# Output projection of a token pair: seven products of quadrant sums in place of eight, weight operands streamed from DRAM

## The chip, the cores and the metric

The kernel runs on one core of a Trainium2 chip. The metric is the device time of one execution in microseconds (us); the median of a few executions is compared. The core's engines run in parallel, each through its own instruction queue in order: TensorE (PE, with PEld for its weight loads), VectorE (DVE), ScalarE (ACT), GpSimd (POOL) and SyncE (SP), which here only issues DMAs.

## The reference

Two linear-attention blocks over the same 2048 tokens (D = 576, 32 heads of 18), mixed by a gate:

```python
def _A_ref(x, wqkv, wo):            # phi(t) = where(t > 0, t + 1, exp(t)) + 1e-6
    kv = einsum("bhsd,bhse->bhde", phi(k), v);  z = phi(k).sum(s)
    o = einsum("bhqd,bhde->bhqe", phi(q), kv) / (phi(q) . z + 1e-6)
    return o.reshape(B, S, D) @ wo
def _B_ref(x, wqkv, w_phi, wo):     # phi(t) = [softmax(t @ w_phi), softmax(-t @ w_phi)] per head
    return (same linear attention).reshape(B, S, D) @ wo
g = sigmoid((x * gate_w).sum(-1))
return g * A + (1 - g) * B
```

## The kernel before, in words

The 2048 tokens are 16 tiles of 128, worked on in pairs. Three stages follow each other: keys and values of block A, keys and values of block B, then the queries of both with the output projection. All matrix products are exact to float32 by splitting each operand into a high and a low part (`split`: ACT copies the high part, DVE or POOL subtracts it for the low one) and multiplying high by high, high by low and low by high. The projections of x already run in seven products of quadrant sums (`strassen`), with x and its sums kept in DRAM and fetched for each pair (`x_fetch`).

The last stage is the loop over `i` at the end of the kernel. In block `i` it merges three sequences by weight: `q_units(i + 1)` (query projection of the next pair: seven units), `tr_units` (transposes of the normalised queries of pair `i` by TensorE) and `out_units` (output projection of pair `i - 1`). `norm` runs at the head of the block, and `num` multiplies the transposed features of block B by its folded key-value matrix. `out_units` of before takes one tile and one half of the 576 output columns at a time: nine row chunks (`ath`/`atl`, `oh`/`ol` are the high and low left operands) times three matmuls of 128x128 by 128x288. Its weights are resident: `WO(s, i)` reads five tiles (`WOt`) that `load_out` fetched once from the DRAM tensors `wod` and `mad`, which `prep_wo`, `prep_out` and `join_out` filled during the stage before.

No order is written out by hand: the code lists the operations, and `Plan` gives each a due time and an order per engine from costs and from when buffers come free (`order`, `run`). So an edit moves instructions on all engines. Tiles named `op` have eleven buffers (`op_tile`); seven hold the query weights (`WQ`) through the last stage. In a row of the profile all operations carry line 354, the line of `emit` that issues them, so they are told apart by tile names.

Of the kernel before, what the change touches and what calls it, by code (L numbers as in the profile page):

```python
# [18 lines left out]
P = 128  # L19
# [339 lines left out]
def tile_gated_mix(ctx, tc, xT, wAk, wAv, wBv, wAq, wkT, wqT, phi, woA, woB, out):  # L359
# [524 lines left out]
    def prep_wo():  # L884
        for i in range(6):
            src = row_tile()[:, :D]
            SP.dma_start(src, woB[:, i, :])
            if i % 2 == 0:
                t = op_tile()
            k = 2 * (i % 2)  # L890
            split(src, t[:, k], t[:, k + 1], G)
            if k:
                SP.dma_start(WO_d[:, i - 1:i + 1], r(t).rearrange("p (i s) n -> p i s n", i=2))
            yield

# [14 lines left out]
    WO_d = dr.tile([P, 6, 2, D], F32, name="wod")  # L910
# [23 lines left out]
    MA_d = dr.tile([D, 2, D], F32, name="mad")  # L934

    def prep_out():
# [27 lines left out]
        for c in range(6):  # L964
            wo, nxt = nxt, load(c + 1) if c < 5 else None
            here = [(a, 2 * c + a) for a in range(2 if c < 5 else 1)]
            k, rows = 2 * (c % 2), 64 * len(here)
            if c == 4:
                two = rr(wk.tile([P, 2, D], F32, name="st", bufs=1))
                hi_lo = two[:, 0], two[:, 1]  # L970
            elif c == 5:
                hi_lo = rr(area[0][:, 1152:1152 + D]), rr(area[1][:, :D])
            else:
                if c % 2 == 0:
                    t = op_tile()
                hi_lo = t[:, k], t[:, k + 1]
# [7 lines left out]
            hv, lv = [v[:rows].rearrange("p (a c) -> p a c", a=2) for v in hi_lo]  # L984
            A.activation(hv, pm[:rows, :, :HB], AF.Copy)
            V.tensor_tensor(lv, pm[:rows, :, :HB], r(hv), op=ALU.subtract)
            if c < 4:
                if c % 2:
                    dst = MA_d[108 * (c - 1):108 * (c + 1)].rearrange("(c a q) s n -> a q c s n", c=2, a=2)
                    for a in range(2):  # L990
                        SP.dma_start(dst[a], r(t[64 * a:64 * a + 54]).rearrange("p (c s) n -> p c s n", c=2))
            elif c == 4:
                for a, gr in here:
                    SP.dma_start(MA_d[54 * gr:54 * gr + 54], r(two[64 * a:64 * a + 54]))
            else:
                for s, v in enumerate(hi_lo):
                    SP.dma_start(MA_d[540:, s], r(v[:36]))
            yield

    def join_out():  # L1000
        for a in range(2):
            plan.after(1)
            SP.dma_start(WO_d[64 * a + 54:64 * a + 64, 0:5], MA_d[378:478].rearrange("(k a q) s n -> a q k s n", a=2, q=10)[a])
        plan.after(1)
        SP.dma_start(WO_d[36:, 5], MA_d[478:570])
# [28 lines left out]
    def both():  # L1034
        yield from prep_wo()
        yield from prep_q1()
        yield from prep_out()
        yield from prep_q2()

    prep = both()  # L1040
    a_done, pend = pend, []
    for n in range(NT // 2):
# [6 lines left out]
        for i, _ in enumerate(strassen(x, WB, TB, HB, two_banks, lambda: uws[0][:, 0], *b_sinks(n, uws, pend))):  # L1049
# [11 lines left out]
            if n + i > 3:  # L1061
                steps(prep)
            if n == NT // 2 - 1 and i == 2:
                join_out()
# [5 lines left out]
    def load_out(k, at):  # L1070
        t = op_tile() if k < 4 else tail_tile()
        WOt[k] = t
        plan.first = at
        if k < 3:
            SP.dma_start(r(t).rearrange("p (i s) n -> p i s n", i=2), WO_d[:, 2 * k:2 * k + 2])
        elif k == 3:
            to = r(t).rearrange("p (i s) n -> p i s n", i=2)
            SP.dma_start(to[:126], MA_d[:252].rearrange("(g p) s n -> p g s n", g=2))
            SP.dma_start(to[126:], MA_d[570:574].rearrange("(g p) s n -> p g s n", g=2))
        else:  # L1080
            SP.dma_start(r(t[:126]), MA_d[252:378])
            SP.dma_start(r(t[126:]), MA_d[574:])

    WOt = {}

    def WO(s, i):
        return WOt[i // 2][:, 2 * (i % 2) + s]
# [75 lines left out]
    def q_units(n, x, uws, c1_tile, then={}):  # L1163
# [29 lines left out]
    def tr_units(t, at, uT):  # L1193
        f, ub = qs.pop(t)
        ath, atl = at
# [17 lines left out]

    def num(uT, at, last):
        ath, atl = at
        oh, ol = ot = [wk.tile([P, KT, 256], F32R, name="vo") for _ in range(2)]
# [10 lines left out]
        for m, p1 in enumerate(pms):  # L1227
            j = 2 * m
            n = 2 if j < 4 else 1
            src = p1[:, :256 * n].rearrange("p (j n) -> p j n", n=256)  # L1230
            A.activation(oh[:, j:j + n], src, AF.Copy)
            V.tensor_tensor(ol[:, j:j + n], src, r(oh[:, j:j + n]), op=ALU.subtract)
            if n == 1:
                A.activation(ath[:64, 3], p1[:64, 256:], AF.Copy)
                V.tensor_tensor(atl[:64, 3], p1[:64, 256:], r(ath[:64, 3]), op=ALU.subtract)
        return ot

    def out_units(t, blk):
        ath, atl = blk["at"]
        oh, ol = blk["ot"]  # L1240
        c = slice(P * (t % 2), P * (t % 2) + P)
        osb = row_tile()[:, :D]
        dst = out[P * at_row(t):P * at_row(t) + P]
        for hf in range(2):
            po = bank_tile()
            cc = slice(HB * hf, HB * hf + HB)
            srcs = [(ath, atl, m, 6 + m) for m in range(3)] + [(oh, ol, j, j) for j in range(KT)] + [(ath, atl, 3, 5)]
            st = []
            for hi, lo, j, i in srcs:
                st += [(hi[:, j, c], WO(0, i)), (hi[:, j, c], WO(1, i)), (lo[:, j, c], WO(0, i))]  # L1250
            for i, (l, w) in enumerate(st):
                PE.matmul(po[:, :HB], l, w[:, cc], start=(i == 0), stop=(i == len(st) - 1))
            A.activation(osb[:, cc], po[:, :HB], AF.Copy)
            if t >= NT - 2:
                SP.dma_start(dst[:, cc], osb[:, cc])
            if hf == 0:
                yield
        if t < NT - 2:
            SP.dma_start(dst, osb)
        yield  # L1260
# [24 lines left out]
    for i in range(NT // 2 + 1):  # L1285
# [4 lines left out]
        if i and i <= NT // 2:  # L1290
            prev["ot"] = num(uT, prev["at"], i >= NT // 2 - 1)
        if i + 1 < NT // 2:
            x = x_fetch(pairs[i + 1])
            if i == 0:
                load_out(3, x["dma"])
                load_out(4, x["dma"])
            if i == 1:
                for k, m in enumerate((1, 4, 6)):
                    load_out(k, x["dma"][m:m + 1])
            uws = [extra_uw if i == 0 else uw_tile(), uw_tile()]  # L1300
            seqs.append((7, .7, q_units(i + 1, x, uws, row_tile)))
# [5 lines left out]
        if i:  # L1307
            seqs.append((4, 1, chain(*[out_units(t, prev) for t in (2 * i - 1, 2 * i - 2)])))
# [83 lines left out]
```

## Time and profile before

| what | value |
|---|---|
| median of 3 runs | 561.49 us (561.21 to 562.13) |
| profiled execution | 562.4 us, span of its instructions 560.7 us |
| PE busy | 551.6 us (98%), 4584 matmuls |
| DVE, ACT, POOL busy | 421.8 (75%), 288.3 (51%), 245.8 us (44%) |
| TensorE clock granted | 1.00 throughout |
| DMA | 96.22 MB, mean 172 GB/s |
| last stage | from about 285 us to the end |

A row of a group reads: line, engine, operation, output tile <- input tiles, shapes, count | busy us, mean ns of one | idle time of the engine ahead of it and what ended it. Matmuls overlap each other, so the mean of one (297 ns) is its latency; the step from one to the next is read from the timeline.

### The profile page before, as it was taken

To read this page: it belongs to the slowest core of one execution; us is meant where nothing else is said; L and a number is where in the kernel's file an instruction comes from. 1 tells how busy PE (TensorE), PEld (TensorE's weight loads), DVE (VectorE), ACT (ScalarE), POOL (GpSimd) and SP (SyncE) were. 2 spreads that over 40 slices of the span, in tenths; PEclk is the share of its full clock that TensorE was granted. 3 is DMA by queue.
4 is the path that set the end of the run, shared out by engine and by line. 5 is a ranking of instruction groups with operands and counts; after the bars stand their busy time and mean duration, and the time that the engine had idled before them with its cause. 6 is when DMAs were issued, how large, how long until landed. Compare 5 with 4: busy or idle time off the path is not lost.

```text
span 560.7 us, 11695 instructions
## 1 busy us (share of the span) xinstructions
PE 551.6 (98%) x4584; PEld 527.7 (94%) x4584; DVE 421.8 (75%) x673; ACT 288.3 (51%) x602; POOL 245.8 (44%) x218
## 2 busy tenths in 40 slices
PE   8999999999999999999999989999999999999997
PEld 8999999999999978999998989898999989899897
DVE  5872678843897997899889998769597795978810
ACT  6666687655645544543355645435443544535421
POOL 6575487632793523363228764214152332424200
PEclk9999999999999999999999999999999999999999
DMA  8739767976759566757759622132322314100001
GB/s 282 272 116 312 252 236 253 338 245 269 273 208 384 184 214 210 250 184 261 284 182 311 247 80 77 48 105 70 106 78 85 97 44 122 51 1 23 31 34 43
DMA packets 38625, 96.22 MB, mean 172 GB/s; under 512 B 4198, under 2 KB 7782, under 8 KB 37034
## 3 DMA queue, kind: packets, MB, share of 16 engines
q1 hardware_dynamic: 38570, 95.47, 50.2%
q8 instruction: 36, 0.59, 0.4%
q14 instruction: 19, 0.16, 0.1%
HBM read 59.64 MB, written 36.70 MB: 172 GB/s over the span
## 4 chain that ended last, share of the span: by engine, by line
PE 83%; DVE 10%; POOL 2%; ACT 2%; issue 1%; DMA 1%; SPq 0%; POOLq 0%; DVEq 0%; ACTq 0%
PE pq L354 35%; PE tr L354 25%; PE bk L354 23%; DVE row L354 3%; DVE dd L354 2%; DVE den L354 1%; DVE mm L354 1%; DVE ss L354 1%; POOL late L354 1%; POOL row L354 1%; DVE at L354 1%; DMA at<-xT 1%; DVE rs L354 1%; ACT row L354 1%; ACT uw L354 0%
## 5 line engine op out<-in xcount | busy, mean ns | idle before, releaser
L354 PE MATMUL pq<-op,x 128*128 128x288 f32 (+1 forms) x636 | 102.6, 297 | 0.0
L354 PEld LDWEIGHTS pq<-op,x 128*128 128x128 f32 x636 | 90.4, 189 | 0.9 <-issue 0.4
L354 PE MATMUL bk<-op,vo 128*128 128x288 f32 x480 | 71.0, 297 | 0.0
L354 PE MATMUL pq<-tail,x 128*128 128x288 f32 (+1 forms) x308 | 66.9, 300 | 0.0
L354 PEld LDWEIGHTS bk<-op,vo 128*128 128x128 f32 x480 | 65.8, 188 | 0.2 <-DVE vo L354 0.2
L354 PE MATMUL pq<-op,xp 128*128 128x288 f32 (+1 forms) x336 | 54.0, 297 | 0.0
L354 PE MATMUL bk<-op,at 128*128 128x288 f32 x288 | 51.3, 301 | 0.0
L354 POOL TENSOR_TENSOR row<-row,z_a 128x576 f32<-128x576 f32 x16 | 22.9, 1429 | 63.3 <-issue 35.7
L354 PEld LDWEIGHTS pq<-tail,x 128*128 128x128 f32 x308 | 49.1, 188 | 1.3 <-issue 0.6
L354 ACT ACTIVATE row<-bk 128x288 f32<-128x288 f32 x38 | 15.6, 411 | 64.4 <-PE bk L354 64.4
L354 PEld LDWEIGHTS pq<-op,xp 128*128 128x128 f32 x336 | 47.5, 188 | 0.2
L354 ACT ACTIVATE row<-row,epsc 128x576 f32<-128x576 f32 x54 | 41.9, 777 | 10.5 <-DVE row L354 9.4
L354 POOL TENSOR_TENSOR row<-row,den 128x378 f32<-128x378 f32 (+1 forms) x32 | 24.6, 789 | 47.8 <-DVE den L354 39.4
L354 DVE TENSOR_REDUCE ss<-uw 128x64 f32<-128x1152 f32 x23 | 31.0, 1350 | 18.5 <-ACT uw L354 17.9
L354 ACT ACTIVATE row<-tr 128x288 f32<-128x288 f32 (+1 forms) x74 | 30.2, 409 | 28.1 <-PE tr L354 27.2
L354 PEld LDWEIGHTS bk<-op,at 128*128 128x128 f32 x288 | 41.7, 189 | 0.4 <-issue 0.4
L354 ACT ACTIVATE uw<-uw 128x1152 f32<-128x1152 f32 x23 | 26.8, 1166 | 23.8 <-DVE uw L354 13.6
L354 POOL TENSOR_TENSOR x<-at,x 128x384 fp32r<-128x384 f32 (+2 forms) x35 | 31.3, 898 | 16.5 <-ACT x L354 14.4
L354 DVE TENSOR_TENSOR row<-row,pq 128x576 f32<-128x576 f32 (+1 forms) x30 | 22.5, 750 | 18.7 <-ACT row L354 14.3
L354 PE MATMUL tr<-op,xv 128*128 128x288 f32 (+1 forms) x204 | 33.7, 302 | 0.0
L354 ACT ACTIVATE uT<-tr 118x512 f32<-118x512 f32 (+1 forms) x48 | 25.9, 559 | 14.6 <-PE tr L354 14.5
L354 DVE TENSOR_TENSOR vo<-row,pq 128x540 f32<-128x540 f32 (+1 forms) x56 | 22.8, 449 | 11.4 <-ACT row L354 10.4
(206 smaller groups left out, 1264.3 us busy)
## 6 DMA issues: line engine op xcount, KB each, us to landing
xp<-s0x SPq DMA_DIRECT2D x12, 512.0 KB
at<-xT SPq DMA_DIRECT2D x18, 320.0 KB
x<-x1x SPq DMA_DIRECT2D x12, 384.0 KB
x<-s2x SPq DMA_DIRECT2D x12, 384.0 KB
s0x<-xp SPq DMA_DIRECT2D x8, 512.0 KB
out<-row SPq DMA_DIRECT2D x14, 288.0 KB
op<-wb SPq DMA_DIRECT2D x3, 1152.0 KB
wod<-op SPq DMA_DIRECT2D x3, 1152.0 KB
```

Source lines behind the costliest of these rows:

```text
L354: fn(*[a.real() if isinstance(a, View) else a for a in args], **{k: v.real() if isinstance(v, View) else v for k, v in kw.items()})
```

## The change

The output projection of a pair is now taken as one product of a 256-token operand by the weights, both cut into quadrants, with seven products of quadrant sums in place of eight (the last 128 of the operand's rows stand apart as a tail). Per pair that is 7 x 12 matmuls and 12 for the tail, 96, where 2 x 2 x 27 = 108 stood. The left operands' sums and splits are made for each pair: four sums and seven splits, on DVE (`fast`, `slow`) for the first pairs and on POOL later. The seven weight operands (high and low, 1152 KB each) are made during the stage before by `prep_o` into DRAM tensors `od0` to `od3` (`O_d`; the tail is `otd`). The first of them stays resident, and the other six are loaded for every pair into `op` tiles. `prep_wo` and `join_out` are gone, `prep_out` runs first and writes plain rows to `mad`. The scaling of block B's features in `norm` (`scale_ub`) is on DVE for all tiles; it was on POOL for the first four.

The core of the diff:

```diff
+    O_OPS = {1: (0, 0), 2: (1, 0), 3: (1, 1), 5: (2, 0), 6: (2, 1), 7: (3, 0), 4: (3, 1)}
+    O_d = [dr.tile([P, 1 if i == 0 else 2, 2, 4, HB], F32, name=f"od{i}") for i in range(4)]
...
+    def prep_o():
...
+        for k in range(4):
+            r1, r2 = nxt
+            ta, tb = wide[k % 2][:, 2], wide[k % 2][:, 3]
+            G.tensor_tensor(ta[:, :HB], r1[:, HB:], r1[:, :HB], op=ALU.subtract)
+            G.tensor_tensor(ta[:, HB:], r2[:, HB:], ta[:, :HB], op=ALU.subtract)
+            put_two(2, k, ta, None)
             yield
...
     def both():
-        yield from prep_wo()
+        yield from prep_out()
         yield from prep_q1()
-        yield from prep_out()
         yield from prep_q2()
+        yield from prep_o()
...
+    def load_o(op):
+        t = op_tile()
+        i, o = O_OPS[op]
+        SP.dma_start(r(t).rearrange("p a b -> p (a b)"), O_d[i][:, o].rearrange("p s k c -> p (s k c)"))
...
-            norm_b(t, *qb[t], ub, (G, V, G if t < 4 else V))
+            norm_b(t, *qb[t], ub, (G, V, V))
...
-        src = chunks(p1)
-        A.activation(ath[:, 0:4, c], src, AF.Copy)
-        V.tensor_tensor(atl[:, 0:4, c], src, r(ath[:, 0:4, c]), op=ALU.subtract)
+        A.activation(ra[:, :, c], chunks(p1), AF.Copy)
...
+    def out_units(i, blk, wo):
+        fast = V if i < 3 or i >= NT // 2 - 1 else G
+        slow = V if i < 2 else G
...
+        L12 = cut(a12, vo(), V)
+        fast.tensor_tensor(s1, a21, a22, op=ALU.add)
+        slow.tensor_tensor(a21, a11, a21, op=ALU.subtract)
+        fast.tensor_tensor(a11, s1, a11, op=ALU.subtract)
+        slow.tensor_tensor(a12, a12, a11, op=ALU.subtract)
+        LS2 = cut(a11, slots[1], fast)
+        LS1 = cut(s1, vo(), slow)
+        split(d, own[:, 0, 2048:2176], own[:, 0, 2176:], V)
...
+        X = bank_tile()
+        mul(X, ops(L11, 1), True)
+        A.activation(ob[0][:, h0], X[:, :HB], AF.Copy)
+        LS3 = cut(a21, slots[0], slow)
+        yield
+        Y = bank_tile()
+        mul(Y, tail(*t1, 0) + ops(L12, 2), True)
+        V.tensor_tensor(ob[0][:, h0], ob[0][:, h0], Y[:, :HB], op=ALU.add)
...
+        mul(X, ops(LS2, 6), False)
...
+        mul(Z, tail(*t2, 1) + ops(LS1, 5), True)
...
+        mul(X, ops(LS3, 7), False)
...
+        mul(X, ops(L22, 4) + tail(*t2, 0), False)
...
+        mul(Z, ops(LS4, 3) + tail(*dd, 1), False)
...
         if i:
-            seqs.append((4, 1, chain(*[out_units(t, prev) for t in (2 * i - 1, 2 * i - 2)])))
+            wo = {op: WO[1] if op == 1 else load_o(op) for op in (1, 2, 6, 5, 7, 4, 3)}
+            seqs.append((7, 1 if i == 6 else 1, out_units(i, prev, wo)))
```

How this stands in the queues is shown at one block in the middle of the last stage, and at the stage's first pair. In the rows, `bk` is an accumulator in PSUM, `at`, `vo` and `row` are operands of the output projection, `x...`, `xp`, `xv` are the fetched operands of the query projection, and the numbers tell buffers apart.

On PE before, at the fourth unit of the query projection in that block (`pq` is its accumulator), one half tile of the output projection begins with resident weights `op_3729`, `tail_3733`, `op_3754`:

```order
L354 MATMUL pq_4831<-op_3371,x3_4675 128x288 x12
L354 MATMUL tr_5071<-ident_138,row_4925 128x128 x4
L354 MATMUL bk_5080<-op_3729,at_4517 128x288 x5
L354 MATMUL pq_4831<-op_3415,xv_4707 128x288 x6
L354 MATMUL pq_4831<-tail_2567,x2_4282 128x288 x2
L354 MATMUL pq_4831<-op_3415,xv_4707 128x288 x6
L354 MATMUL pq_4831<-tail_2567,x2_4282 128x288 x2
L354 MATMUL bk_5080<-op_3729,at_4517 128x288
L354 MATMUL bk_5080<-tail_3733,at_4517 128x288 x3
```

On PE now, at the same units: the end of product 2 (`op_4912`), product 6 (`op_4988`) and product 5 (`op_5147`).

```order
L354 MATMUL bk_5063<-op_4912,vo_5043 128x288 x4
L354 MATMUL pq_5101<-op_2487,xp_4750 128x288
L354 MATMUL bk_5003<-op_4988,op_4084 128x288 x12
L354 MATMUL tr_5164<-ident_138,late_3932 118x128 x3
L354 MATMUL pq_4919<-op_3385,x3_4766 128x288 x12
L354 MATMUL bk_5191<-tail_3896,row_5036 128x288 x3
L354 MATMUL pq_4919<-op_3406,xv_4823 128x288 x4
L354 MATMUL bk_5191<-op_5147,vo_5072 128x288 x12
```

Between two readings of resident tiles nothing had to arrive; now each product reads a tile loaded for it. After product 5 stand 12 matmuls of the query projection, four transposes and seven matmuls more, and then on PE now products 7 (`op_5171`), 4 (`op_5235`) and 3 (`op_5293`):

```order
L354 MATMUL bk_5003<-op_5171,op_4084 128x288 x12
L354 MATMUL pq_5101<-tail_2496,x4_4881 128x288
L354 MATMUL pq_5101<-op_3431,x4_4881 128x288 x6
L354 MATMUL pq_5101<-tail_2496,x4_4881 128x288 x2
L354 MATMUL tr_5303<-ident_138,late_3932 118x128 x4
L354 MATMUL tr_5311<-ident_138,late_3932 118x128 x4
L354 MATMUL bk_5003<-op_5235,vo_5145 128x288 x12
L354 MATMUL bk_5003<-tail_3896,row_5036 128x288 x3
L354 MATMUL tr_5343<-ident_138,late_3932 118x128 x3
L354 MATMUL pq_5351<-op_2434,xu_4949 128x288 x12
L354 MATMUL pq_5373<-op_2446,x1_5070 128x288 x2
L354 MATMUL bk_5191<-op_5293,op_4084 128x288 x12
```

On SP before, the same stretch of the block holds fetches of x and a store of `out` only:

```order
L354 DMA x1_4969<-x1x3_662 128x768
L354 DMA xp_5023<-s0x3_713 128x1024
L354 DMA out<-row_4940 128x576
L354 DMA x3_5078<-s1x3_751 128x512
L354 DMA xv_5110<-x2x3_800 128x512
L354 DMA x2_5116<-x3x4_875 128x256
L354 DMA x4_5175<-s2x3_826 128x768
```

On SP now:

```order
L354 DMA x1_5070<-x1x3_662 128x768
L354 DMA op_5147<-od2_3039 128x2304
L354 DMA xp_5153<-s0x3_713 128x1024
L354 DMA op_5171<-od3_3090 128x2304
L354 DMA x3_5197<-s1x3_751 128x512
L354 DMA op_5235<-od3_3090 128x2304
L354 DMA xv_5250<-x2x3_800 128x512
L354 DMA x2_5257<-x3x4_875 128x256
L354 DMA op_5293<-od1_3180 128x2304
L354 DMA x4_5309<-s2x3_826 128x768
```

Four weight loads have come between the fetches of x. Of the eleven `op` buffers seven hold query weights, one the first weight operand and one (`op_4084`) left operands, so two are left for the loads: `op_5147` takes the buffer of `op_4912`, `op_5171` that of `op_4988`, `op_5235` that of `op_5147`, `op_5293` that of `op_5171`.

On DVE before, behind the first product of block B's features (`num`), stand the subtractions that give the low parts (`vo<-tr`, `vo<-bk`, `at<-tr`) among the norms:

```order
L354 TENSOR_TENSOR vo_4162<-tr_4055,vo_4089 128x512
L354 TENSOR_TENSOR vo_4162<-tr_4056,vo_4089 128x512
L354 TENSOR_REDUCE ss_4177<-uw_3976 128x64
L354 RECIPROCAL rs_4193<-ss_4177 128x64
L354 TENSOR_TENSOR vo_4162<-bk_4057,vo_4089 128x256
```

On DVE now, in the same place, for the first pair: sums (`st`, `at`) and splits (`vo`, `op_4084`) of the left operands, and the scaling of features (`late`), which POOL did before.

```order
L354 TENSOR_TENSOR op_4084<-at_3944,op_4084 128x512
L354 TENSOR_TENSOR dd_4239<-dd_4239,rs_4179 128x64
L354 SCALAR_TENSOR_TENSOR den_4330<-dd_4239 128x32
L354 TENSOR_TENSOR late_3932<-uw_4015,rs_4155 128x72
L354 RECIPROCAL den_4330<-den_4330 128x32
L354 SCALAR_TENSOR_TENSOR rs_4179<-den_4330,gate_269,rs_4179 128x64
L354 TENSOR_TENSOR late_3932<-vo_3952,rs_4179 128x10x54 x2
L354 TENSOR_TENSOR late_3932<-vo_3952,rs_4179 128x72
L354 TENSOR_TENSOR vo_4275<-st_4216,vo_4275 128x512
L354 TENSOR_TENSOR op_4084<-at_3944,op_4084 128x512
L354 TENSOR_TENSOR row_4325<-row_4325,pq_4260 128x576
L354 TENSOR_TENSOR vo_4361<-at_3944,vo_4361 128x512
```

The low parts of one tile's chunks have given way to sums and splits of 512 columns each for the pair.

More of the change, by code (lines that the diff above doesn't have):

```diff
@@ L998, in prep_out @@
-            yield
[L1000 to L1005, printed above, removed]
+            ma = row_tile()[:, :D]
+            A.activation(ma[:rows].rearrange("p (a c) -> p a c", a=2), pm[:rows, :, :HB], AF.Copy)
+            for a, gr in here:
+                n = 54 if gr < 10 else 36
+                SP.dma_start(MA_d[54 * gr:54 * gr + n], ma[64 * a:64 * a + n])
@@ L1236, in num @@
[L1236 to L1259, printed above, removed]
+        A.activation(ra[:64, 3], pms[2][:64, 256:], AF.Copy)
```

217 lines of the change are left out of this document (139 added, 78 removed).

## The prediction

> **What bounds the kernel now.** I read the page first: how busy each engine is, and which engines make up the chain that ended last.
>
> ```profile
> PE 551.6 (98%) x4584; PEld 527.7 (94%) x4584; DVE 421.8 (75%) x673; ACT 288.3 (51%) x602; POOL 245.8 (44%) x218
> PE 83%; DVE 10%; POOL 2%; ACT 2%; issue 1%; DMA 1%; SPq 0%; POOLq 0%; DVEq 0%; ACTq 0%
> ```
>
> A busy TensorE need not be the bound, so I next asked whom it waited for, and looked at the last stage, which the change rewrites, in stretches from one `num` to the next.
>
> ```profile
> PE tr L354 <- DVE vo L354: 1.8, 2, 1.1
> ...
> core 0: us, PE busy (x) PEld busy (x) DVE busy (x) ACT busy (x) POOL busy (x), PEclk, DMA share, GB/s
> 383.28:417.32 34.04, 34.01 (x261) 32.52 (x261) 26.51 (x48) 15.55 (x31) 11.56 (x11) 1.00 0.27 84
> 451.35:485.38 34.03, 34.02 (x262) 32.53 (x261) 26.47 (x48) 15.66 (x31) 11.52 (x11) 1.00 0.27 80
> ```
>
> The longest wait of TensorE in total is 1.8 us, and block after block of the last stage takes the same 34.04 us with TensorE full. DVE has 7.5 us of slack in a block, POOL 22, and the DMA engines are at 27%. So TensorE bounds each block, at a fixed clock, and whatever matmul goes shortens it, as long as nothing else takes its place. Only at the start of the stage is that otherwise:
>
> ```profile
> 285.00:340.00 55.00, 52.33 (x385) 48.34 (x382) 53.31 (x92) 30.52 (x67) 35.28 (x33) 1.00 0.59 195
> ```
>
> There DVE works 53.3 of 55 us and TensorE loses 2.7.
>
> **What is removed.** The output projection is these three groups:
>
> ```profile
> L354 PE MATMUL bk<-op,vo 128*128 128x288 f32 x480 | 71.0, 297 | 0.0
> L354 PE MATMUL bk<-op,at 128*128 128x288 f32 x288 | 51.3, 301 | 0.0
> L354 PE MATMUL bk<-tail,at 128*128 128x288 f32 x96 | 18.4, 297 | 0.0
> ```
>
> 864 matmuls, 108 for each of eight pairs. Now there are 96 a pair, 768; 96 go. The step of one I take from the end of the run, where nothing but these stands on TensorE, and that of a transpose from a run of eight a little before:
>
> ```profile
> 535.25 1.03 PE L354 MATMUL tr<-ident,late 128*118 128x128 f32 x8
> 536.03 1.04 PE L354 MATMUL bk<-op,at 128*128 128x288 f32 x6
> ...
> 549.73 1.36 PE L354 MATMUL bk<-op,at 128*128 128x288 f32 x9
> ...
> 556.90 0.56 PE L354 MATMUL bk<-op,at 128*128 128x288 f32 x3
> ```
>
> From 549.73 to 556.90 start 54 matmuls: 7.17 / 54 = 0.1328 us each. Eight transposes take 536.03 - 535.25 = 0.78, so 0.098 each. The change removes 96 x 0.1328 = **12.75 us** of TensorE's path, 1.59 a block: a block comes to 34.04 - 1.59 = 32.45 us if nothing is late.
>
> **What is added: the stream of weights.** This is the dispute. Six operands of 1152 KB come from DRAM for each pair, into two rotating buffers. What such a load costs is read from these rows: sizes, then three stretches in which the queue was full, then one load alone.
>
> ```profile
> op<-wq SPq DMA_DIRECT2D x3, 1152.0 KB
> xp<-s0x SPq DMA_DIRECT2D x12, 512.0 KB
> xv<-x2x SPq DMA_DIRECT2D x12, 256.0 KB
> x<-s1x SPq DMA_DIRECT2D x12, 256.0 KB
> x<-x3x SPq DMA_DIRECT2D x12, 128.0 KB
> ...
> DMA packets 1321, 4.04 MB, mean 404 GB/s; under 512 B 145, under 2 KB 145, under 8 KB 1192
> ...
> DMA packets 666, 3.69 MB, mean 369 GB/s; under 512 B 57, under 2 KB 57, under 8 KB 351
> q1 hardware_dynamic: 664, 3.67, 101.1%
> ...
> DMA packets 204, 1.73 MB, mean 346 GB/s; under 512 B 17, under 2 KB 17, under 8 KB 17
> ...
> 119.27 0.33 SPq L354 DMA_DIRECT2D at<-xT  x1
> 122.58 0.43 DVE L354 TENSOR_TENSOR at<-at 128x256 f32<-128x256 f32 x1 [1.37 <-DMA at<-xT]
> ```
>
> The stretches are 168 to 178 us, 263 to 273 (the three loads of query weights, of the same shape as the new ones, with small ones beside them), and 265 to 270 within it. The lone load of 320 KB took 122.58 - 119.27 = 3.31 us from issue to the instruction that waited; 0.33 MB at 404 GB/s is 0.81 of that, so about 2.5 us are fixed.
>
> Now the block that the change's part shows. From the end of product 2 to the start of product 3 its queue holds 113 matmuls and 18 transposes: 113 x 0.1328 + 18 x 0.098 = 16.8 us. In that time four operand loads and four fetches of x have to pass, 4 x 1152 + 512 + 256 + 256 + 128 KB = 5.90 MB. At 404 GB/s that is 2.5 + 14.6 = 17.1 us, at 369 it is 2.5 + 16.0 = 18.5. So the stream is 0.3 to 1.7 us late in a block. The first load of the four shows it alone: between the ends of products 2 and the start of 5 are 32 matmuls and 3 transposes, 4.5 us, and 1152 KB need 2.5 + 1.18 / 0.404 = 5.4. The rest of the block (product 3 to the next product 2) has two loads for some 15 us and gives slack, but only the two buffers' worth can be taken ahead. Blocks 1 to 6 have both streams; in blocks 7 and 8 the query weights' buffers are free and no x is fetched. I take the middle, 1.0 us, for six blocks: **+6.0 us** (1.8 to 10.2). On SP an operand load waits for the matmuls that free its buffer, and what stands behind it are fetches of x, which have most of a block until they are read; these waits I cost at nothing.
>
> [...]
>
> **What is added: operands on DVE, POOL and ACT.** In a middle block DVE loses the low parts of before and gets splits and sums. The prices:
>
> ```profile
> L354 DVE TENSOR_TENSOR vo<-tr,vo 128x512 fp32r<-128x512 f32 x12 | 7.6, 677 | 0.2 <-POOL late L354 0.2
> L354 DVE TENSOR_TENSOR vo<-bk,vo 128x256 fp32r<-128x256 f32 x6 | 2.4, 406 | 0.0
> L354 DVE SCALAR_TENSOR_TENSOR row<-tr,row 128x288 f32<-128x288 f32 x14 | 5.8, 453 | 17.4 <-ACT row L354 16.0 <-ACT gate L354 1.3
> L354 DVE TENSOR_TENSOR late<-uw,rs 128x540 f32<-128x540 f32 x24 | 17.3, 721 | 0.8
> L354 DVE TENSOR_TENSOR late<-uw,rs 128x72 f32<-128x72 f32 x12 | 3.3, 272 | 0.0
> L354 POOL TENSOR_TENSOR xp<-at,xp 128x512 fp32r<-128x512 f32 x8 | 11.9, 1489 | 5.9 <-PE tr L354 3.3 <-ACT xp L354 2.6
> L354 POOL TENSOR_TENSOR row<-row,z_a 128x576 f32<-128x576 f32 x16 | 22.9, 1429 | 63.3 <-issue 35.7 <-DVE row L354 22.4 <-DVE den L354 4.4
> ```
>
> DVE loses 4 x 0.677 + 2 x 0.406 = 3.5 and gains, in blocks 3 to 6, two splits of 512, one of 384 (0.55, between the rows for 256 and 512), four of 128 (0.3 as the row for 72), one of 256 and three additions of 288 from PSUM: 1.35 + 0.55 + 1.2 + 0.4 + 1.35 = 4.85. So 26.5 + 1.3 = 27.8 of 32.45 us. POOL gets eight operations of 512: 8 x 1.489 = 11.9, 23.4 in all. ACT gets some eight copies at half a microsecond each on its 15.6. TensorE covers all three; no cost, and if that cover goes it is a rival below.
>
> At the start of the stage it is not covered. `scale_ub` of four tiles goes from POOL to DVE, 4 x (2 x 0.721 + 0.272) = 6.9, and the first pair's sums and splits are all on DVE: four sums and six splits of 512 at 0.677 are 6.8, the seventh split, the smaller ones and the additions from PSUM about 3.3 more. Off go the low parts of four tiles and of the first `num`, 6 x 0.677 + 2 x 0.406 = 4.9. That is about +12 us on an engine with 1.7 idle in 55. What of it reaches TensorE lies between 0 (it has the next pair's query projection to run ahead with, and today a DVE that is full for 55 us costs it only 2.7) and 10.3 (12 less the idle). I take the value near the row of today: **+3 us**, after which DVE's 4.6 us a block of slack make up the rest.
>
> **The stage before.** `prep_o` puts on POOL, four times over, five operations of 288 columns and three of 576, and one of 576 more: by the 1.43 us of the row for 576 and half of it, 4 x 7.9 + 1.4 = 33 us. Its stores go out in runs of 1152 bytes. This has to fit here:
>
> ```profile
> 200.00:250.00 50.00, 50.00 (x445) 45.36 (x444) 42.79 (x63) 22.57 (x39) 18.84 (x10) 1.00 0.67 212
> 250.00:290.00 40.00, 40.00 (x381) 39.24 (x381) 35.00 (x49) 16.55 (x29) 13.92 (x9) 1.00 0.71 248
> ```
>
> POOL is idle for 57 of these 90 us, the DMA engines for 28, and TensorE never waits; DVE is even relieved of the low parts of `mad`. TensorE has no wait to lose there, so nothing can be gained, and I cost it at nothing; if POOL's leavings or the stores reach into the start of the last stage, it comes on top of the +3 there, by at most the 7.1 us that the 10.3 still allow.
>
> **The sum.** -12.75 + 6.0 + 3.0 = -3.75 us. Against the profiled execution (562.4, its span 560.7 and 1.7 around it) that is 558.65; that execution lay 0.9 over the median, so against 561.49 the forecast is **557.7 us**. Its own range, with the ends of both terms taken so far as they are likely together: 550.5 (stream 1.8, start 0) to 562.0 (10.2 and 3).
>
> **The rivals.**
>
> *All of it is hidden.* If the loads run at the upper rate with their fixed part overlapped (the queue is rarely empty), and TensorE bridges the start, the full 12.75 comes: 561.49 - 12.75 = 548.7. For it: 14.6 us at 404 GB/s are less than the 16.8 there are. Against: DVE at the start.
>
> *The stream becomes the bound, and the kernel is slower.* At 346 GB/s the stretch takes 2.5 + 17.1 = 19.6, 2.8 late, six times: 561.49 - 12.75 + 16.5 + 3 = 568.2. It decides from (12.75 - 3) / 6 = 1.6 us a block on: 5.90 / (16.8 + 1.6 - 2.5) = 371 GB/s. That is right between my rows, which is why my chance for faster is not high. For it also: the fetches of x are of smaller packets than the operands. Against: two of the three rows, and that a late product also gives the loads behind it time. [...]
>
> *POOL and DVE get in each other's way.* A place in a middle block, and DVE's side of it:
>
> ```profile
> 412.50 3.36 POOL L354 TENSOR_TENSOR row<-uw,z_b 128x576 f32<-128x576 f32 x2 [0.43 <-ACT uw L354]
> ...
> L354 DVE TENSOR_TENSOR row<-uw,z_b 128x576 f32<-128x576 f32 x15 | 13.3, 884 | 0.0
> ```
>
> Two POOL operations take 3.36 us where two of 1.43 would take 2.86: a DVE operation with both inputs in SBUF ran beside them. If the two engines strictly take turns, a middle block has POOL's 23.4 and DVE's two-input work: 2 x 0.884, 4 x 0.721, 2 x 0.272, the new splits (3.1) and about 3 of smaller ones, 11.3 in all, 34.7 against 32.45 us. Four blocks (3 to 6) by 2.3 give 9 us: 557.7 + 9 = 566.7, slower. Against: an overlap at the ends of operations, and today's block has 20 of 34 us without any stretch on TensorE. [...]
>
> That the change does not do what it says is excluded by the queue on PE: 96 matmuls a pair stand there.
>
> **Chances.** Forecast 0.45, all hidden 0.18, stream as the bound 0.22, the shared ports 0.10, something in the stage before or at the end 0.05. A measurement can tell about 0.2% from no change, 1.1 us: 560.4 to 562.6. Of the forecast's 0.45 I put 0.38 below and 0.06 within, 0.01 above; with the others: faster 0.57, same 0.07, slower 0.36. The range takes in the full gain and the stream as the bound, 548.5 to 568.5; outside are the worse halves of the last cases, some 1.5 in 10.
>
> **What would show it.** TensorE with 96 matmuls fewer, and middle blocks of 32.5 us plus the lateness. Right: waits of TensorE named after a DMA of `op<-od`, short, at products 5, 7, 4 and 3, 1 us a block, none in blocks 7 and 8; a DMA share of some 0.8 to 0.9; 2 to 4 us lost between 290 and 350 us, to DVE. Wrong: blocks of 32.5 without waits (the first rival), waits of 2 us and more a block after DMAs (the second), or waits after POOL's `op`, `vo` or `at` (the third).

## The result, and the profile after

The changed kernel takes **591.89 us** (589.36 to 595.16, four runs) against 561.48: 1.054 times as long, 95% interval 1.048 to 1.061. The forecast was 557.7. Its profiled execution took 589.9, span 588.2.

The page of the changed kernel ("after" from here on): the engines' busy time, the granted clock in tenths over 40 slices, and the chain of work that ended last.

```profile
PE 553.7 (94%) x4488; PEld 523.2 (89%) x4488; DVE 469.0 (80%) x736; ACT 323.3 (55%) x685; POOL 328.7 (56%) x280
...
PEclk9999999999999999899999899999998998999799
...
PE 49%; DVE 24%; DMA 17%; POOL 4%; issue 3%; ACT 2%; SPq 1%; ACTq 0%; POOLq 0%; DVEq 0%
```

The 96 matmuls are gone (4488 for 4584), yet TensorE is busy longer than before, and its share of the chain falls from 83 to 49%. Two things came: waits, and a clock that is no longer 1.00 all along. The three largest waits of TensorE in after (what it waited for, us in total, times, longest):

```profile
PE bk L354 <- DMA op<-od: 9.1, 9, 2.0
PE bk L354 <- DVE op L354: 6.5, 4, 3.2
PE pq L354 <- DVE tail L354: 3.5, 1, 3.5
```

The last stage of after, from one `num` to the next (the last row ends with the run), then the last three blocks of before. Columns as in the prediction.

```profile
323.53:361.89 38.36, 32.73 (x231) 30.09 (x230) 35.50 (x66) 22.73 (x47) 16.57 (x14) 0.96 0.61 211
361.89:397.95 36.06, 33.43 (x250) 31.24 (x249) 33.63 (x57) 19.02 (x39) 18.37 (x15) 1.00 0.80 276
397.95:435.65 37.70, 33.86 (x249) 31.14 (x248) 31.22 (x54) 20.06 (x41) 22.67 (x19) 1.00 0.73 256
...
473.27:510.39 37.12, 34.87 (x251) 32.75 (x250) 32.00 (x53) 19.41 (x40) 21.35 (x18) 0.95 0.71 255
510.39:542.58 32.19, 31.38 (x240) 29.63 (x239) 31.81 (x48) 18.88 (x37) 23.34 (x18) 1.00 0.97 381
542.58:565.74 23.16, 20.13 (x131) 17.97 (x131) 20.92 (x42) 11.64 (x30) 10.70 (x9) 0.85 0.91 356
565.74:588.20 22.46, 18.89 (x137) 16.92 (x136) 9.39 (x16) 7.69 (x18) 6.83 (x5) 0.99 0.25 97
```
```profile
485.38:519.44 34.06, 34.04 (x262) 32.58 (x262) 27.59 (x49) 15.93 (x32) 11.34 (x11) 1.00 0.05 19
519.44:541.19 21.75, 20.93 (x161) 19.26 (x160) 12.23 (x25) 8.02 (x19) 2.78 (x3) 1.00 0.07 28
541.19:560.70 19.51, 16.26 (x123) 14.92 (x122) 1.94 (x4) 3.26 (x8) 0.00 (x0) 1.00 0.13 46
```

One block, 510.39 to 542.58, takes 32.19 us for a promised 32.45, but it holds 240 matmuls where the middle ones hold 245 to 251, so it is no clean confirmation; a clean one follows below. The four middle blocks take 36.1 to 37.7, the last two 1.4 and 3.0 more than before, and the first `num` comes at 323.5 for 316.5.

**One late load, seen whole.** SP's queue, TensorE and the DMA share in after:

```profile
487.57 0.32 SPq L354 DMA_DIRECT2D op<-od  x1
488.10 0.32 SPq L354 DMA_DIRECT2D xp<-s0x  x1
489.70 0.32 SPq L354 DMA_DIRECT2D op<-od  x1
```
```profile
486.74 0.80 PE L354 MATMUL bk<-op,vo 128*128 128x288 f32 x4
...
494.39 2.26 PE L354 MATMUL bk<-op,vo 128*128 128x288 f32 x12 [1.66 <-DMA op<-od]
```
```profile
484.00:485.00 1.00, 0.81 (x7) 0.58 (x5) 1.00 (x3) 0.57 (x1) 1.00 (x2) 1.00 0.00 0
...
487.00:488.00 1.00, 1.00 (x9) 1.00 (x9) 0.35 (x1) 0.38 (x1) 1.00 (x1) 1.00 0.00 0
...
493.00:494.00 1.00, 0.00 (x0) 0.00 (x0) 0.96 (x3) 0.87 (x2) 0.74 (x1) 1.00 1.11 463
```

From 484 to 488 the DMA engines do nothing: both buffers are held by products. At 487.5 one product ends, the load into its buffer goes out at 487.57, a fetch of x of 512 KB half a microsecond behind it, and the product that needs the load starts at 494.39, 6.8 us later. The engines are not slow then: 406, 417, 370 and 463 GB/s in the four microseconds from 490 on, against the 404 that the prediction took. Some 2.1 MB pass from 488 to the start of the product, 1.18 of them the load that it needs; the fetch of x and the next load take their share. What lacks is the time in which the queue stood empty.

**One stall and the clock behind it**, after in stretches of 1 us:

```profile
442.00:443.00 1.00, 0.01 (x1) 0.02 (x1) 1.00 (x2) 0.00 (x0) 0.78 (x1) 1.00 0.30 120
...
445.00:446.00 1.00, 1.00 (x7) 1.00 (x6) 0.92 (x2) 0.06 (x1) 0.96 (x1) 0.50 0.00 0
446.00:447.00 1.00, 1.00 (x6) 1.00 (x6) 1.00 (x2) 1.00 (x3) 0.00 (x0) 0.50 0.90 230
...
448.00:449.00 1.00, 1.00 (x10) 1.00 (x9) 0.04 (x1) 0.11 (x1) 1.00 (x2) 1.00 0.00 0
```
```profile
441.16 1.62 POOL L354 TENSOR_TENSOR at<-at 128x512 f32<-128x512 f32 x1
441.59 1.34 DVE L354 TENSOR_TENSOR op<-at,op 128x128 fp32r<-128x128 f32 x1
...
442.99 0.40 PE L354 MATMUL bk<-op 128*128 128x288 f32 x1 [2.04 <-DVE op L354]
```

TensorE stands for 2.0 us to 443.0, and from 444.5 to 447.9, 3.41 us, its clock is 0.50: 1.7 us more are lost. It waits for a short split on DVE, which takes 1.34 us beside a POOL operation of the new sums; the mean of that split over the run is 0.68 us, and 0.32 in the run below that has no sums. After has five such places (240, 332, 444, 496 and, two long, 550), six windows of 3.41 us at half clock; TensorE was busy in nearly all of that time and lost 9.6 us by it. Before has none.

### The profile page after: what moved, and what is told of

Same layout as the page of the kernel before. It is cut to its first block, busy times and chain, and to the rows that moved or that the text cites. A ratio compares the mean times of both kernels' runs of the same rounds, so it can differ in the third digit from the quotient of the medians.

```text
span 588.2 us, 11971 instructions
## 1 busy us (share of the span) xinstructions
PE 553.7 (94%) x4488; PEld 523.2 (89%) x4488; DVE 469.0 (80%) x736; ACT 323.3 (55%) x685; POOL 328.7 (56%) x280
## 4 chain that ended last, share of the span: by engine, by line
PE 49%; DVE 24%; DMA 17%; POOL 4%; issue 3%; ACT 2%; SPq 1%; ACTq 0%; POOLq 0%; DVEq 0%
PE pq L354 20%; PE tr L354 15%; PE bk L354 14%; DMA op<-od 8%; DVE row L354 5%; DMA od<-st 3%; DVE ss L354 3%; DVE den L354 3%; DVE dd L354 3%; DVE late L354 2%; DVE mm L354 2%; DMA wq<-st 2%; DMA od<-at 1%; DVE op L354 1%; DVE rs L354 1%
## 5 line engine op out<-in xcount | busy, mean ns | idle before, releaser
L354 PE MATMUL pq<-op,x 128*128 128x288 f32 (+1 forms) x636 | 106.0, 299 | 4.6 <-DVE tail L354 3.5
L354 PE MATMUL bk<-op 128*128 128x288 f32 x384 | 62.4, 303 | 11.8 <-DVE op L354 6.5
L354 PEld LDWEIGHTS bk<-op 128*128 128x128 f32 x384 | 53.5, 189 | 16.9 <-DVE op L354 8.1
L354 PE MATMUL bk<-op,vo 128*128 128x288 f32 x288 | 47.2, 311 | 4.5 <-DMA op<-od 3.9
L354 PEld LDWEIGHTS pq<-op,xp 128*128 128x128 f32 x336 | 49.0, 193 | 0.0
L354 PEld LDWEIGHTS bk<-op,vo 128*128 128x128 f32 x288 | 42.1, 199 | 6.3 <-DMA op<-od 2.5
L354 ACT ACTIVATE row<-tr 128x288 f32<-128x288 f32 (+2 forms) x76 | 30.7, 406 | 27.9 <-PE tr L354 26.0
L354 ACT ACTIVATE at<-tr 128x512 f32<-128x512 f32 (+2 forms) x44 | 22.8, 521 | 24.3 <-PE tr L354 24.2
L354 DVE TENSOR_TENSOR at<-at 128x256 f32<-128x256 f32 (+2 forms) x40 | 27.0, 701 | 7.2 <-DMA at<-xT 6.8
L354 DVE TENSOR_TENSOR late<-uw,rs 128x540 f32<-128x540 f32 (+1 forms) x45 | 30.8, 691 | 0.8
```

Source lines behind the costliest of these rows:

```text
L354: fn(*[a.real() if isinstance(a, View) else a for a in args], **{k: v.real() if isinstance(v, View) else v for k, v in kw.items()})
```

## The experiments

All edits are to the changed kernel unless said. Times are medians of four runs; before measured 561.6 to 562.4 beside them. Kernels with half-clock windows (below) scatter by up to 2% from run to run, those without by 0.4%; differences of 3 us between the former are not read.

**Leaving out one part each.** First the stream.

```diff
-            wo = {op: WO[1] if op == 1 else load_o(op) for op in (1, 2, 6, 5, 7, 4, 3)}
+            wo = {op: WO[1] for op in (1, 2, 6, 5, 7, 4, 3)}
```

> All seven products read the one resident operand (op1): no operand is loaded per pair, so the 55 MB of the stream and the waits for buffers go; everything else stays. The theory that the stream makes the lateness (waits of TensorE after op<-od, 9.1 us in all, with the clock that falls behind them): the middle blocks come back from 36.1-37.7 us to about 32.5, and the time falls by some 18 to 22 us to 570-574. The theory that the new operands on DVE and POOL make it: the waits after DVE's op and tail stay, middle blocks stay above 35 us, 583-590.

574.18 us, 17.7 less. A middle block of it:

```profile
459.62:491.85 32.23, 32.23 (x249) 30.95 (x249) 31.62 (x51) 19.18 (x38) 20.94 (x18) 1.00 0.25 76
```

Without loads this block is full on TensorE, with 249 matmuls for 262 before, and takes what was forecast, with DVE at 31.6; the four middle blocks take 32.1 to 33.1 for 36.1 to 37.7. So the stream makes nearly all that they lose, 18.0 us together. Directly seen of that are 7.0 us of waits after loads and two half-clock windows, 3.4 us. Waits after DVE fall too, from 4.6 us to 0.8; how the late loads lengthen those was not followed. Then the preparation.

```diff
-        yield from prep_o()
...
-        SP.dma_start(r(t).rearrange("p a b -> p (a b)"), O_d[i][:, o].rearrange("p s k c -> p (s k c)"))
+        SP.dma_start(r(t), WQd[op if op in (7, 4, 3) else 7])
```

> The preparation of the seven operands (prep_o) is left out; the stream loads as many bytes from query-weight operands that lie in DRAM anyway. The theory that the stage before pays for prep_o: the 7 us that the first num comes later than in the kernel before (323.5 against 316.5) shrink to 1 or 2, and the whole falls by 5 to 9 us to 583-587. The rival (prep_o hides beside a stage in which POOL and the DMA engines are half idle, and the delay is from the start of the last stage): 590-592, no change.

579.26 (575.0 to 581.6), 12.6 less, more than either theory gave; the first `num` comes at 313.2, 10.3 earlier. Then the sums.

```diff
-        fast.tensor_tensor(s1, a21, a22, op=ALU.add)
...
-        LS2 = cut(a11, slots[1], fast)
-        LS1 = cut(s1, vo(), slow)
+        LS2 = cut(a11, slots[1], fast) if i == 1 else lefts(slots[1])
+        LS1 = L12
...
-        LS3 = cut(a21, slots[0], slow)
+        LS3 = L11
...
-        LS4 = cut(a12, slots[1], slow)
+        LS4 = LS2
```

(The four sums go for all pairs.)

> The four sums and the splits of the sums' operands are done for the first pair only; later products 6, 5, 7 and 3 read left operands that lie there. POOL loses its eight operations of 512 elements a middle block and DVE those of pairs 2, 7 and 8. The theory that DVE and POOL, which hold each other up, make the lateness: DVE's time in a middle block falls from 31-33 to about 27 us, waits after DVE go, middle blocks lose 2 to 4 us each, total 572-580. The theory that the stream makes it: the waits after op<-od stay or grow, 586-591.

578.45, 13.4 less, but its four runs fall into two groups, 574 and 583, so the size is rough. DVE's groups in after, then in this run:

```profile
L354 DVE TENSOR_TENSOR late<-uw,rs 128x540 f32<-128x540 f32 x30 | 26.5, 883 | 0.8
L354 DVE SCALAR_TENSOR_TENSOR den<-dd 128x32 f32<-128x32 f32 x16 | 7.6, 475 | 0.5
```
```profile
L354 DVE TENSOR_TENSOR late<-uw,rs 128x540 f32<-128x540 f32 x30 | 21.6, 721 | 1.1
L354 DVE SCALAR_TENSOR_TENSOR den<-dd 128x32 f32<-128x32 f32 x16 | 3.2, 202 | 0.5
```

The same DVE operations, not touched by the edit, take 0.88 and 0.48 us beside POOL's new work and 0.72 and 0.20 without it. All three together:

> All three of these edits at once. If stream, operands and preparation are all that was wrong, 96 matmuls fewer are left, and the time is 549-553 us (561.5 - 12.75, and up to 4 for what DVE still does for the first pair). If something else costs too (order of the work, smaller splits, additions from PSUM), it stays above 556.

556.25, at a clock of 1.00 throughout. A middle block has TensorE full and DVE at the 28 us that the prediction counted:

```profile
448.35:481.04 32.69, 32.52 (x249) 31.00 (x249) 28.22 (x53) 17.45 (x36) 10.98 (x11) 1.00 0.28 83
```

**Bytes, rate or buffers.** The loads kept, with an eighth of their bytes (`n = 288` of 2304 columns a partition):

> Every load of an operand stays, with its buffer and its place in the queue, but brings one eighth of its bytes (144 KB in place of 1152), and the products use that part again and again. The theory that the bytes make the lateness (rate of the DMA engines): nearly the whole 17.7 us that leaving out the stream gave, 574-577. The theory that the two rotating buffers and the fixed part of a load make it (the load can't start before a product frees its buffer): half of it or less, 581-588.

575.98: like no stream. The expectation gave such a time to the rate of the DMA engines; but a short load would be there in time in either case, so the run does not tell rate from time. Four half-size buffers (the pool of operand buffers cut to 9 whole ones, two loads an operand):

```diff
-        return wp.tile([P, 4, w], F32R, name="op", bufs=11)
+        return wp.tile([P, 4, w], F32R, name="op", bufs=9)
...
+            ts = [wp.tile([P, 4 * HB], F32R, name="oh", bufs=4) for h in range(2)]
```

> The two rotating buffers become four of half the size, each operand comes in two loads (k 0-1, k 2-3), and a product goes through its operand half by half, so a buffer comes free 1.6 us into a product; same bytes, same sums. The theory that the rotation makes the lateness: the waits after op<-od shrink from 9 us to 3 or less, with the half-clock windows behind them, 580-586. The theory that the rate of the DMA engines makes it: no change, 589-593, or slower by the extra loads.

641.41, a miss of its own making: with 9 whole buffers, which the stages before share, the first `num` comes at 380.5. Blocks 3 to 5 of it take 35.4 to 36.5, about 1.4 less than in after, which may be the finer rotation. Three buffers of full size:

```diff
-                WO[1] = load_o(1)
+                WO[1] = WQ[1].rearrange("p a b -> p (a b)").rearrange("p (s k c) -> p s k c", s=2, k=4)
```

> Product 1 reads a query-weight operand that is there anyway, so its own resident buffer is free and three rotate for the stream in place of two; the same six loads a pair, the same bytes, the same matmuls. The theory that the two buffers leave a load too little time: waits after op<-od fall from 9 us to 3 or less, blocks of 33-34 us for 37.6, 578-583. The theory that the DMA engines' rate is what lacks: blocks stay above 36 us, 588-593.

575.91, and no wait of TensorE after `op<-od`. The same six loads a pair with the same bytes: so at the rate that there is, what lacked was the time that two buffers leave a load. Since that run reads a foreign operand in product 1, the complete form streams all seven:

```diff
-                WO[1] = load_o(1)
...
-            wo = {op: WO[1] if op == 1 else load_o(op) for op in (1, 2, 6, 5, 7, 4, 3)}
+            wo = {op: load_o(op) for op in (1, 2, 6, 5, 7, 4, 3)}
```

> Complete and correct by its work: no operand of the output projection stays resident, all seven are loaded for each pair, and the buffer so gained makes three rotate in place of two. 9.4 MB more traffic than in the changed kernel. The theory that the rotation of two buffers made the stream's 16 to 18 us: 575-580, with no wait of TensorE after op<-od worth speaking of. The theory that bytes count as such (a seventh load, at a mean of 276 GB/s already): 586-596.

**575.30 us** (1.024 of before, 1.019 to 1.029): a sixth more in the stream and 16.6 us less than the change as made. A block of it, at 348 GB/s without a late load:

```profile
458.25:490.49 32.24, 32.24 (x249) 30.96 (x248) 31.37 (x51) 19.15 (x38) 20.69 (x19) 1.00 0.92 348
```

**What makes the preparation dear.** Without its POOL work (high parts stored twice), then without its stores:

> prep_o keeps its loads, its copies on ACT and all its stores, but its 33 us of sums and low parts on POOL are left out (the high parts are stored twice). The theory that POOL, which holds up DVE's two-input operations, makes the 12.6 us that leaving out prep_o gave: 578-583. The theory that its loads and stores on the DMA queue make them: 588-592.

> prep_o keeps its loads and its work on POOL and ACT, but stores nothing; the stream loads as many bytes from query-weight operands. The theory that POOL beside DVE makes the 12.6 us: 588-592. The theory that the stores (runs of 1152 bytes, DMA share 1.0 from 230 to 320 us) make them: 578-583.

585.73 (580.2 to 589.0) and 589.44: 6.2 of the 12.6, and 2.5, which lies within the scatter of after. Neither moves the first `num` to the front (323.4 and 324.8; without `prep_o` 313.2). Where POOL's work hurts can be seen in after:

```profile
235.94 1.40 POOL L354 TENSOR_TENSOR at<-late,at 128x576 fp32r<-128x576 f32 x1
235.99 1.97 DVE L354 TENSOR_TENSOR uw<-uw,mm 128x576 f32<-128x576 f32 x1
...
237.31 1.92 POOL L354 TENSOR_TENSOR st<-uT,st 128x576 fp32r<-128x576 f32 x1
...
237.99 1.86 DVE L354 TENSOR_TENSOR tail<-late,tail 64x576 fp32r<-64x576 f32 x1
...
239.92 0.82 PE L354 MATMUL pq<-op,x 128*128 128x288 f32 x2 [3.49 <-DVE tail L354]
```

The second one's group in before:

```profile
L354 DVE TENSOR_TENSOR tail<-late,tail 64x576 fp32r<-64x576 f32 x2 | 2.0, 1023 | 0.0
```

Two of `prep_o`'s low parts run beside two DVE operations that take 1.97 and 1.86 us (their groups in before have means of 0.98 and 1.02), and TensorE waits 3.5 us, with a half-clock window behind it. But with POOL's work gone the delay of `num` stays. Both runs keep the loads, ACT's copies and the tiles (`uT`, `late`, `st`) that `prep_o` holds to its end and the last stage wants next; which of these it is stays open.

**The start of the stage.** `scale_ub` of four tiles back on POOL (`(G, V, V)` to `(G, V, G if t < 4 else V)`):

> scale_ub of the first four tiles goes back from DVE to POOL. The theory that DVE is what the start of the last stage waits for: 6.9 us less on DVE there, the first block (38.4 us) comes down by 3 to 6 us, and its half-clock window goes: 585-589. The rival (POOL's 1.5 us operations hold DVE up by as much as they relieve it, or the start waits for something else): 590-595.

587.24 (585.4 to 591.4, where after has 589.4 to 595.2), 4.7 less. With the three parts left out as well:

> No stream, no preparation, no sums (as in the run with all three left out, 556.3 us), and scale_ub of the first four tiles on POOL as in the kernel before. That run's first block took 35.3 us where 30.4 were to be had. The theory that DVE's scale_ub at the start makes it: 551-553. The rival (the splits of the first num's operands on DVE, and the last block of 23 us): 555-557.

555.60, against 556.25: no difference. The first block falls from 35.3 to 32.7, and the next three grow by 3.2 together. So what is left over in that run is not `scale_ub`; what it is stays open.

**The sums alone:** stream and preparation left out, sums kept.

> No stream (all products read op1) and no preparation, but all sums and splits stay: against the run with all three left out (556.3) it prices the left operands' sums alone. The theory that DVE, held up by POOL, makes them dear: 563-570, most of it in the first block and the last two, where no work of the next pair covers them. The rival (they cost only where the stream is late as well): 556-559.

568.21, 12.0 above the run without sums: 3.9 in the first block, 6.5 in the seventh pair's, 2 in all the others. In the seventh pair's block stand two half-clock windows, some 3 of the 6.5 us.

**Mended versions.** Seven streamed operands with `scale_ub` on POOL; that with `prep_o`'s low parts on DVE; the low parts alone; and these with the last two pairs' sums all on DVE.

> Seven streamed operands on three buffers, and scale_ub of the first four tiles on POOL. If the 4.7 us that this gave before add to the gain of the buffers: 571-575. If both came out of the same first block: 575-580.

> As the kernel with seven streamed operands and scale_ub on POOL, and prep_o's low parts (some 13 operations) on DVE in place of POOL. The theory that POOL's long operations beside DVE make prep_o's price: 3 to 6 us faster than without this edit, 566-571. The rival (DVE is the fuller engine in that stage, 42.8 of 50 us busy): same or slower, 573-580.

> Seven streamed operands on three buffers, prep_o's low parts on DVE, scale_ub as in the changed kernel. The lows on DVE gave 11 us on top of the version with scale_ub on POOL. If that is their own price: 564-568. If that version only carried half-clock windows that a shifted order set off or took away, and the buffers' gain is all there is: 570-575.

> As the one before, and the sums and splits of the last two pairs all on DVE, POOL left out there. In the seventh pair's block TensorE has 17.6 us of work and takes 23.5, while POOL's operations of 1.3 to 1.8 us stretch DVE's beside them (0.28 to 1.25, 0.22 to 1.31). The theory that this lock makes the 6 us: 1 to 4 us faster than without the edit. The rival (DVE's work as such fills the block, and five operations more make it longer): same or up to 3 slower.

583.33, 572.02, 583.26 and 582.70, where seven streamed operands alone gave 575.30. These edits do not add, and the first and the third came out slower than either of their theories had them. None of the four has late loads to speak of; the three slow ones have middle blocks of 36 us where the other and the one without edits have 33. A block of the one with the low parts alone, and the wait in it:

```profile
428.99:465.55 36.56, 34.42 (x249) 32.46 (x248) 31.96 (x53) 19.49 (x41) 22.64 (x19) 0.95 0.85 306
```
```profile
434.50 1.26 POOL L354 TENSOR_TENSOR at<-at 128x512 f32<-128x512 f32 x1
434.53 1.27 DVE L354 SCALAR_TENSOR_TENSOR den<-dd 128x32 f32<-128x32 f32 x1
...
436.39 0.40 PE L354 MATMUL bk<-op 128*128 128x288 f32 x1 [1.86 <-DVE op L354]
```

With DVE at 32 us of work in a block of 33, it matters where the planner puts the one short split that product 1 waits for (`op<-at` 128x128): here behind a row of `norm`'s operations, one of which takes 1.27 us beside a POOL operation and 0.20 (above) without. The longest such wait, 3.2 us, stands in the first block of after and of the run with seven streamed operands alike. In the seventh pair's block, where the run with all seven streamed takes 23.5 us, the last edit gives 21.1 for 23.6, so POOL's long operations are part of what makes that block long; the last block grows by 0.8, and the whole time moves by less than the scatter. In the run with seven streamed operands one sees it at work:

```profile
539.62 1.75 POOL L354 TENSOR_TENSOR at<-at 128x512 f32<-128x512 f32 x1
540.14 1.31 DVE L354 TENSOR_TENSOR late<-uw,rs 128x72 f32<-128x72 f32 x1
...
542.12 1.29 POOL L354 TENSOR_TENSOR op<-at,op 128x512 fp32r<-128x512 f32 x1 [0.75 <-ACT op L354]
...
542.24 1.25 DVE L354 SCALAR_TENSOR_TENSOR rs<-den,gate,rs 128x64 f32<-128x64 f32 x1
```

Operations with means of 0.22 and 0.28 us in the run without sums take 1.31 and 1.25 here and end within 0.1 us of the POOL operation beside them. No complete version got under the kernel before; the fastest, with both edits, is 572.02 (571.0 to 575.2), hardly apart from seven streamed operands alone (572.4 to 579.2).

**The clock by itself**, in a program that does nothing else.

> Another program: 36 runs of 96 matmuls (about 12.7 us each) with waits of TensorE between them of about 0.8 to 3.8 us, made by DVE operations of 100 to 2850 elements; nothing else runs, no DMA beside it. If TensorE's granted clock falls by what TensorE idles, as the traces of the changed kernel look: waits under 1.3 us are followed by no half clock, waits of 2 us by half clock for 3.4 us in about half of the cases (where one window holds 1.8 us of it), waits over 3 us nearly always. If it falls for another reason (DMA traffic, several engines at once): no half clock here at all.

Two neighbouring stretches of it:

```profile
20.07 12.96 PE L34 MATMUL acc<-zero,left 128*128 128x288 f32 x96 [1.00 <-DVE left L38]
35.34 14.45 PE L34 MATMUL acc<-zero,left 128*128 128x288 f32 x96 [2.31 <-DVE left L38]
```

After a wait of 1.00 us 96 matmuls take 12.96 us, after one of 2.31 us 14.45. Over all 35 waits, with the granted clock read in stretches of 0.25 us:

```
wait of TensorE, us    waits   followed by 0.50
1.00 to 1.53             9       0
1.79                     3       1 (one window)
2.05                     3       0
2.31 to 3.09            11      11 (one window each)
3.35 to 3.87             9       9 (eight of them two windows)
```

A window is 3.41 us, and all begin on one grid of 3.413 us that runs through the whole program (36.02, 53.09, 70.15, ...). No large DMA runs after the first 20 us, and DVE is the only other engine at work: idle time of TensorE is enough. What counts is how much of it falls into one grid window: the waits of 2.05 us are cut by a window's end, leave 1.82 to 1.84 us in one window and halve nothing, while one of 1.79 us lies whole in a window and does. In the traces of the changed kernel and of the three runs that leave out one part it is the same, up to their last matmuls: every full-clock window with 1.92 us or more of idle time was followed by one at 0.50, none with 1.30 or less was, and from 1.41 to 1.86 it went either way. So 2 us of waiting may cost 2 or 3.7, as it falls.

## Why the prediction was wrong

Left out one after the other, the parts make up the whole gap: 548.7 (561.5 less 12.75), +7.5 that stays with none of the three (556.25), +12.0 the sums (568.2), +6.0 the preparation (574.2), +17.7 the stream (591.9). In another order the shares differ (leaving out only the preparation gives 12.6); that waits which follow each other share windows of the clock is a likely reason, not shown. Between forecast and result lie 34.2 us: the stream made 11.7 of them, and the terms put at +3 and at nothing the other 22.5.

- **-12.75 for 96 matmuls: right.** The block without late loads takes 32.2 us for 32.45, with 249 matmuls for 262.
- **The stream, +6.0 with a range to 10.2: the step that failed first.** It measured 17.7. The sum took the four loads as one full queue of 5.9 MB against 16.8 us of TensorE. With two buffers each load begins only when a product ends, and the queue stands empty before: 4 us in the place shown. The rate of 404 GB/s was near enough (414 on average over the four microseconds shown), and 371 GB/s as the deciding point was the wrong question. The rival "the stream becomes the bound" priced the stream at 16.5, close to the 17.7, but by a rate of 346 GB/s; the nearness is luck, since a third buffer takes the cost away with more bytes. The sentence that the two buffers' worth can be taken ahead had the fact in it, and its cost was not worked out load by load.
- **Middle blocks' DVE, POOL and ACT at nothing: wrong by itself only a little, wrong in company.** The 27.8 us were right for DVE's own work (28.2 without the new sums); beside them on POOL it is 31 to 33, of 32.5. The rival that POOL and DVE get in each other's way named the two engines, and priced it at +9 in blocks 3 to 6; there the sums cost 3 us as long as nothing else is late, and the dear places are the first block and the seventh pair's, which it did not name. With the stream they cost more there: the stall at 443 us is such a place. That the two strictly take turns, or share ports, as the chances call it, no run shows. What the runs show is DVE's operations taking longer beside POOL's: the operation `late` of 128x72 has a mean of 0.22 us in the run without sums and took 1.31 under a POOL operation of 1.75.
- **The start, +3: too small.** The first `num` is 7 us late and the first block 8 longer than forecast. `scale_ub` is some 4.7 of the whole time; the run with three parts left out still has 4.9 over in that block.
- **The stage before at nothing, "TensorE has no wait to lose there": wrong, 6.0 to 12.6.** That POOL and the DMA engines were idle half the time said nothing of the DVE operations beside POOL, behind which TensorE waits 3.5 us in the place shown; why the first `num` is late is open, and the tiles that the preparation holds are one candidate.
- **The last two pairs at nothing: a term that was missing.** They have no next projection to cover the sums, and lose 1.4 and 3.0 us against before instead of winning 1.6 each. Without sums, stream and preparation they win 0.7 together instead of 3.2, so the sums are not all of it.
- **The clock as fixed: missing too.** Its six windows cost 9.6 us of TensorE's time, a third of the 30.4 us that the kernel lost; they are part of the prices above, not on top of them. No row of before could show it: there TensorE, once under way, never waits for 2 us.

## What to carry to other kernels

Cost a stream through rotating buffers load by load: the time from the end of the use that frees a buffer to the next use of it, against the fixed part (2.5 us by the prediction's estimate from a lone load of 3.31) and the bytes of a load and of what is queued beside it. The rate over a stretch is not enough while the queue may stand empty, and a third buffer was worth as much here as seven eighths of the bytes. Where an engine beside the bound is filled to 97%, as DVE was here, short operations that the bound waits for came late in one order or another (TensorE waited 1.9 to 3.2 us for one short split); and a wait of TensorE of 2.0 us, at 443 us in after, cost 1.7 us over its length.

## What the runs showed of the hardware

- TensorE's granted clock was 1.00 or 0.50 and nothing between, at 0.50 for windows of 3.41 us on a grid of 3.413 us (six of them in after, and the program that does nothing else). In after and the three runs that leave out one part, 1.92 us or more of idle time in one window halved the next in every case, 1.30 us or less in none. In the program that does nothing else all 20 waits of 2.31 us or more were followed by a window at 0.50, and none of the nine of 1.53 us or less.
- The core moved 381 GB/s over a block of 32 us in after (510.39 to 542.58, operand loads and stores of `out` mixed) and 421 GB/s over one of 23.5 in the run with seven streamed operands.

The last rate stands in this row of the run with seven streamed operands:

```profile
524.57:548.07 23.50, 18.77 (x132) 15.46 (x131) 21.86 (x43) 12.06 (x30) 12.05 (x10) 1.00 1.02 421
```
